# The 64-row tails of the key, value and first dense weights: one load each, from a source that names the rows twice, instead of two loads each

## The chip, the cores and the metric

The kernel runs on one core of a Trainium2 chip. The metric is device microseconds of one execution. Before the change the median of three runs is 150.07 us (149.78 to 150.78).

## What is computed

The input `x` is one sequence of 2048 tokens with 448 features, in bf16. It is normalised, and two branches read the normalised rows; their results are added to `x`.

```
xn  = layernorm(x)
q, k, v = xn @ wqkv                      # 16 heads of 28
phi(t)  = [softmax(t @ w_phi), softmax(-(t @ w_phi))]
kv  = sum_s phi(k)^T v ;  z = sum_s phi(k)
o   = (phi(q) kv) / (phi(q) z + 1e-6)
A   = o @ wo
h   = xn @ w1 + b1                       # w1: 448 x 1792
B   = (h * tanh(softplus(h))) @ w2       # mish
out = x + A + B
```

## The kernel before

**Tokens and features.** The 2048 tokens are 16 tiles of 128 rows, taken in 8 pairs `u`. 448 features are three chunks of 128 and a rest of 64. The transposed rows of a pair, `xnT[:, u]`, have seven chunks: three of the even tile, three of the odd tile, and one (chunk 3) that holds the rest of the even tile in partitions 0 to 63 and the rest of the odd tile in partitions 64 to 127. A matmul against that shared chunk therefore needs the last 64 rows of the weight in both halves of the partitions. Weights are kept as `[128, 4, n]`: chunks 0 to 2 hold rows 0 to 383, and chunk 3 holds rows 384 to 447 twice, once in each half. The projections (`run`, line 433) use one half of the partitions at a time.

**Loads.** `Wkv` is one buffer with the key weights in its first 448 columns and the value weights in the next 448. Rows 0 to 383 come by `load_main` (line 310), `Wk` and `Wv` apart. The last 64 rows, key and value together (64 rows of 1792 bytes), come by `load_tail` (line 315), once for each half. `W1` has the same two parts: `load_main`, and a tail of 64 rows of 3584 bytes for each half. Loads are issued on two queues: SP's (called q1 in the profile) and ACT's (q10). DMA transposes (of `wqkv` into `WqT`, of `xn` into `xnT`, of `Eq` into `EqT`) go through SP's queue too.

**Order.** A list of step names, `ORDER`, sets the order in which the work of all five engines is recorded; each engine runs its own part in that order and waits on semaphores. An engine never runs a later step ahead of one that waits. The steps that matter here are:

- `lba`, `lkma`, `lvma`: the loads of `b1` (14 rows of 256 bytes), of `Wk`'s and of `Wv`'s first 384 rows, on ACT's queue.
- `lktb`: the tail of `Wkv`, lower half on SP's queue and upper half on ACT's.
- `lx1s`, `lx3s`, `lx2s`, `lx4s`, `lx6s`: pieces of `x`; `lps`: `w_phi`; `lqT0` to `lqT3`: transposes of the query weights. All on SP's queue.
- `z5`, `z6`: eleven matmuls of zeros at the start (line 402).
- `wtk0b`, `wtk1b`: TensorE transposes of the key weights (line 585). `wtk0b` reads chunks 0 and 1, `wtk1b` chunks 2 and 3, so it waits for the tail. ACT and DVE each move half of the result out of PSUM; then `wmk0a` and `wmk1a` (line 609) multiply it with `w_phi`.
- `xh3d`, `xh2a`, `xt3a`: TensorE transposes of normalised rows (lines 536 and 520), right behind `wtk1b`.
- `v1Aa`, `v1Ha`: the first projections (line 433); the first of them waits for `Wv`.
- `l1ms`, `l1ts`: `W1`'s main part, and its tail in two loads, both on SP's queue.
- `f0.1H`: the first step of the first dense layer, with chunk 3 of `W1`. It waits for `W1`'s main part and for its tail.

Of the kernel before, what the change touches and what calls it, by code (L numbers as in the profile page):

```python
# [5 lines left out]
ACT = mybir.ActivationFunctionType  # L6
# [6 lines left out]
D = 448  # L13
# [26 lines left out]
class Program:  # L40
# [46 lines left out]
    def dma(self, eng, fn, r=(), w=(), tag=""):  # L87
        return self.op(eng, fn, r, w, dma=True, tag=tag)
# [84 lines left out]
def bass_parallel_sum__linear_kernel_hedgehog__dense_activation_mish__prompt_kernel(  # L173
    nc, A_x, A_wqkv, A_w_phi, A_wo, B_x, B_w1, B_b1, B_w2, out
):
    es = ExitStack()
    with es:
        _kernel(es, nc, A_x, A_wqkv, A_w_phi, A_wo, B_w1, B_b1, B_w2, out)


ORDER = """
zero lx1s lx3s lba st2d lkma lps pw pp st6d lktb lx2s table z5 pi lvma st3a z6 pm lx4s rt3a st7d rs3a xm3a lqT0 rt2p
xm2d b1 xn3d wtk0b bdp wtk1b xh3d st5d xh2a st4d lqT2 xt3a wmk0a wmk1b lqT3 rs2p v1Aa lqT1 st8d v1Ha v3Bd lx6s st9a
v1Ba pk v3Hd k3B xn2d v3Ad rs4p qd k3H xt2m xn4d k3A st14d st15d st12d rs7p lx0s st11d k1H k1A wmq0a wmq1a k1B v2Bd
st13d k2A rs6a k2H v2Ad xn7p st10d q1H xt4m l1ms k2B xn6p v2Hd q1A q2B q1B q2H st1d st0d xt7m q2A e2 v4Ad rs5a v4Hd
# [20 lines left out]
def _kernel(es, nc, A_x, A_wqkv, A_w_phi, A_wo, B_w1, B_b1, B_w2, out):  # L206
    def sb(name, shape, dtype):
        return es.enter_context(nc.sbuf_tensor(name, shape, dtype))
# [21 lines left out]
    W1 = sb("W1", [P, 4, F], BF16)  # L230
# [3 lines left out]
    Wkv = sb("Wkv", [P, 4, 2 * D], BF16)  # L234
# [60 lines left out]
    op, dma = pg.op, pg.dma  # L295
# [4 lines left out]
    HALF = ((0, 64), (64, 128))  # L300
# [9 lines left out]
        dma(eng, lambda e: e.dma_start(dst[:, 0:3, :], src[0:384, :].rearrange("(c p) f -> p c f", p=P)),  # L310
            w=[(name, 0)], tag="ld" + name)

    def load_tail(engs, name, dst, src):
        for i, ((lo, hi), eng) in enumerate(zip(HALF, engs)):
            dma(eng, lambda e, lo=lo, hi=hi: e.dma_start(dst[lo:hi, 3, :], src[384:448, :]),
                w=[("Wt", i) if name == "Wkv" else (name, 1 + i)], tag="ld" + name)

    def load_qT(g, eng):
        dma(eng, lambda e: e.dma_start_transpose(WqT[:, g, 0:D], A_wqkv[:, g * GP:g * GP + P]), w=[("WqT", g)],
# [576 lines left out]
    def add(name, fn, *args):  # L896
        steps[name] = lambda: fn(*args)
# [52 lines left out]
    for eng, c in (("SP", "s"), ("ACT", "a")):  # L950
# [4 lines left out]
        add(f"l1m{c}", load_main, eng, "W1", W1, B_w1)  # L955
        for name, fn in (("p", load_phi), ("b", load_b1), ("2", load_w2), ("o", load_wo)):
            add(f"l{name}{c}", fn, eng)
    for engs, c in ((("SP", "SP"), "s"), (("SP", "ACT"), "b"), (("ACT", "ACT"), "a")):
        add(f"lkt{c}", load_tail, engs, "Wkv", Wkv, A_wqkv[:, D:3 * D])
        add(f"l1t{c}", load_tail, engs, "W1", W1, B_w1)  # L960
    for g in range(G):
        add(f"lqT{g}", load_qT, g, "SP")
    add("b1", bias_T)
# [59 lines left out]
```

## Time and profile before

| | |
|---|---|
| Median of three runs | 150.07 us (149.78 to 150.78) |
| The profiled execution's own time | 149.63 us |
| Its span, first to last instruction | 147.4 us |
| TensorE (PE) busy | 143.1 us, 97% of the span |
| VectorE (DVE) busy | 101.8 us, 69% |
| ScalarE (ACT) busy | 77.0 us, 52% |
| GpSimd (POOL) busy | 39.4 us, 27% |
| DMA, SP's queue (q1) | 38896 packets, 16.09 MB, 51.3% of 16 engines |
| DMA, ACT's queue (q10) | 1052 packets, 0.91 MB, 2.1% of 16 engines |

Some 2.2 us of the execution's own time lie outside the span. A row of the timeline has the start, the length (both in us), the engine, the line of the kernel, the operation, what it writes and reads, and a count; in brackets stands how long the engine was idle before and what ended that. In the chain of waits a row has start, length, and what the end of the program depended on in that time. A DMA row has the packets, the megabytes and the time that the packets took as a share of 16 DMA engines over the stretch asked for.

### The profile page before, as it was taken

The page shows a single profiled execution, that of the slowest core. Times are in us where ns is not written, and L with a number is a line of the kernel's source. Part 1 is how long each engine was busy: PE and PEld are TensorE (multiplying, and loading weights), DVE is VectorE, ACT ScalarE, POOL GpSimd, SP SyncE. Part 2 cuts the span into 40 slices and gives each one's busy share as a digit, 9 for nine tenths or more (in the row PEclk, how much of TensorE's full clock was granted, in tenths as well). Part 3 has the DMA queues.
Part 4 walks back from the last instruction along what each step waited for, and adds up shares of the span by engine and source line. Part 5 has one row for each costly group of instructions (what it writes and reads, how often), then busy time and mean ns, then how long its engine had stood idle before and what let it go on. Part 6 is the DMA issues. An engine that isn't in the chain of part 4 may idle for free.

```text
span 147.4 us, 3868 instructions
## 1 busy us (share of the span) xinstructions
PE 143.1 (97%) x1668; PEld 74.1 (50%) x1668; DVE 101.8 (69%) x227; ACT 77.0 (52%) x98; POOL 39.4 (27%) x54
## 2 busy tenths in 40 slices
PE   7799999999999999999999999999999999999993
PEld 2275555554445545444544446555555545547452
DVE  0898996989997921306999848998997499303522
ACT  3999999989889987996667575000000000000000
POOL 6334283399999990000000000000000000000000
PEclk9999999999999999999999999999999999999999
DMA  4995899995998195399707311015032004500313
GB/s 133 296 274 169 156 350 112 198 202 79 157 203 224 26 163 112 61 190 242 232 4 133 67 32 35 0 24 99 8 57 67 0 4 104 145 0 0 129 64 122
DMA packets 39964, 17.23 MB, mean 117 GB/s; under 512 B 33932, under 2 KB 39180, under 8 KB 39948
## 3 DMA queue, kind: packets, MB, share of 16 engines
q1 hardware_dynamic: 38896, 16.09, 51.3%
q10 hardware_dynamic: 1052, 0.91, 2.1%
q8 instruction: 13, 0.21, 0.6%
q14 instruction: 3, 0.02, 0.0%
HBM read 7.02 MB, written 1.84 MB: 60 GB/s over the span
## 4 chain that ended last, share of the span: by engine, by line
PE 93%; DMA 4%; SPq 1%; DVE 1%; issue 0%
PE PS L433 51%; PE PS L860 29%; PE PS L877 7%; DMA Wkv<-in_A_wqkv_dram 4%; PE PS L754 3%; PE PS L681 2%; PE PS L609 1%; SPq L307 1%; PE PS L585 0%; DVE x_all L824 0%; SPq L330 0%; PE PS L536 0%; PE PS L520 0%; DVE x_all L846 0%
## 5 line engine op out<-in xcount | busy, mean ns | idle before, releaser
L433 PE MATMUL PS<-xnT,W 64*128 64x512 bf16 x392 | 44.8, 376 | 0.0
L860 PE MATMUL PS<-W,actT 128*128 128x448 bf16 (+1 forms) x224 | 42.7, 351 | 0.0
L731 ACT ACTIVATE actT<-PS,b1T 128x1024 bf16<-128x1024 f32 x28 | 30.0, 1113 | 9.3 <-PE PS L433 9.2
L860 PEld LDWEIGHTS PS<-W,actT 128*128 128x128 bf16 x224 | 21.6, 98 | 20.6 <-issue 1.1
L433 PEld LDWEIGHTS PS<-xnT,W 64*128 64x128 bf16 x392 | 18.3, 94 | 21.0 <-issue 0.3
L662 POOL TENSOR_TENSOR actT<-actT,rSk 128x896 bf16<-128x896 bf16 x16 | 26.6, 1700 | 4.8 <-DVE rSk L660 4.8
L824 DVE TENSOR_TENSOR x_all<-PS,x_all 128x448 bf16<-128x448 f32 (+1 forms) x16 | 9.1, 614 | 13.9 <-PE PS L877 8.5
L658 DVE TENSOR_REDUCE Sk<-actT 128x32 f32<-128x896 bf16 x16 | 16.6, 1040 | 0.0
L650 ACT ACTIVATE actT<-PS 128x896 bf16<-128x896 f32 x16 | 13.8, 932 | 0.3 <-PE PS L433 0.2
L433 PE MATMUL PS<-Wkv,xnT 64*128 64x448 bf16 x112 | 13.2, 349 | 0.0
L770 DVE COPY Sq<-PS 128x16 f32<-128x16 f32 x32 | 4.0, 168 | 13.2 <-PE PS L754 13.2
L433 PE MATMUL PS<-Wpk,xnT 64*128 64x448 bf16 x112 | 13.1, 349 | 0.0
L433 PE MATMUL PS<-Wpq,xnT 64*128 64x448 bf16 x112 | 12.7, 349 | 0.0
L471 DVE BATCH_NORM_STATS2 stats<-x_all 128x6 f32<-128x448 bf16 x14 | 8.5, 606 | 3.5 <-DMA x_all<-in_A_x_dram 3.5
L778 DVE TENSOR_TENSOR v_all<-v_all 128x464 f32<-128x464 f32 x16 | 10.3, 643 | 0.6
L774 DVE TENSOR_TENSOR v_all<-PS,Sq 128x464 f32<-128x464 f32 x16 | 10.3, 641 | 0.5
L781 DVE TENSOR_TENSOR xn<-v_all,rden 128x448 bf16<-128x448 f32 x16 | 10.0, 625 | 0.6
L776 DVE TENSOR_TENSOR v_all<-PS,Sq 128x464 f32<-128x464 f32 x16 | 10.1, 630 | 0.0
L712 ACT ACTIVATE actT<-PS 128x896 bf16<-128x896 f32 x10 | 8.4, 925 | 0.6 <-PE PS L433 0.5
L527 DVE CAST v_all<-PS 128x896 bf16<-128x896 f32 x6 | 6.5, 1080 | 3.0 <-PE PS L433 3.0
L433 PEld LDWEIGHTS PS<-Wkv,xnT 64*128 64x128 bf16 x112 | 5.4, 94 | 5.0
L433 PEld LDWEIGHTS PS<-Wpq,xnT 64*128 64x128 bf16 x112 | 5.4, 94 | 5.1 <-ACT actT L731 0.2
(85 smaller groups left out, 121.0 us busy)
## 6 DMA issues: line engine op xcount, KB each, us to landing
W<-in_B_w_dram SPq DMA_DIRECT2D x1, 1568.0 KB, 8.2
out_dram<-x_all SPq DMA_DIRECT2D x7, 224.0 KB, 2.2
W<-in_B_w_dram SPq DMA_DIRECT2D x1, 1344.0 KB, 6.8
x_all<-in_A_x_dram SPq DMA_DIRECT2D x4, 224.0 KB, 2.9
x_all<-in_A_x_dram SPq DMA_DIRECT2D x2, 448.0 KB, 5.1
Wkv<-in_A_wqkv_dram ACTq DMA_DIRECT2D x2, 336.0 KB, 5.1
Wo<-in_A_wo_dram SPq DMA_DIRECT2D x2, 336.0 KB, 4.3
W<-in_B_w_dram SPq DMA_DIRECT2D x2, 224.0 KB, 3.6
```

The source lines that it names most:

```text
L433: ins = e.matmul(o, lhs(c, k), rhs(c, k), start=first and n == at[par][0], stop=last and n == at[par][-1])
L650: op("ACT", lambda e, s=s: e.activation(E_of(u)[:, s, :, :], two(b, D), ACT.Exp, scale=1.0 if s == 0 else -1.0), r=[pb(b), pb(b + 1)], w=[ ...
L658: op("DVE", lambda e: e.tensor_reduce(Sk[u][:, s, :], Eh(), AX.X, ALU.add), r=[("E", u, s)], w=[("Sk", u, s)], tag=f"Sk{u}.{s}")
L662: op("POOL", lambda e: e.tensor_tensor(Eh(), Eh(), ap_on(rSk[u][:, s, 0:1], [[1, 2 * H], [0, DH]]), ALU.mult), r=[("E", u, s), ("rSk", u, ...
L731: op("ACT", lambda e: e.activation(actT[:, fc, q * 1024:(q + 1) * 1024], bank(b, 2), ACT.Mish, bias=b1T[:, fc:fc + 1]), r=[("b1T",), pb(b) ...
L774: op("DVE", lambda e: e.tensor_tensor(tv(t1[i]), num(0), sx(1), ALU.mult), r=[pb(b), pb(b + 1), ("Sq", i, 1)], w=[("t1", i)], tag=f"ta{t}")
L776: op("DVE", lambda e: e.tensor_tensor(tv(t2), num(1), sx(0), ALU.mult), r=[pb(b), pb(b + 1), ("Sq", i, 0)], w=[("t2",)], tag=f"tb{t}")
L778: op("DVE", lambda e: e.tensor_tensor(t1[i], t1[i], t2, ALU.add), r=[("t1", i), ("t2",)], w=[("t1", i)], tag=f"tc{t}")
L781: op("DVE", lambda e: e.tensor_tensor(o_sb[(t // 2) % 2][:, t % 2, :].rearrange("p (h d) -> p h d", d=DH), t1[i][:, :, 0:DH], ap_on(rden[i ...
L824: op("DVE", lambda e: e.tensor_tensor(x_all[:, t, 0:n], bank(b)[:, 0:n], x_all[:, t, 0:n], ALU.add), r=[pb(b), ("x", t)], w=[("out", t)], ...
L860: ins = e.matmul(bank(b)[:, 0:width(t)], actT[:, fc, tok(t)], W2[:, fc, 0:width(t)], start=first and fc == 0, stop=last and fc == FC - 1)
L877: ins = e.matmul(bank(b)[:, 0:w], oT_of(u)[lo:hi, cc * P:(cc + 1) * P], Wo[lo:hi, cc, 0:w], start=first and n == at[par][0], stop=last and ...
```

## The change

The tail of a weight is loaded by one DMA that writes all 128 partitions. Its source has three dimensions, 2 by 64 by the row, and the step of the first is zero, so that the same 64 rows are read twice. The destination has 128 partitions as its first dimension. `Wkv`'s tail is now issued by ACT alone (`lkta` in the place of `lktb`), and `W1`'s, as before, by SP.

```diff
-zero lx1s lx3s lba st2d lkma lps pw pp st6d lktb lx2s table ...
+zero lx1s lx3s lba st2d lkma lps pw pp st6d lkta lx2s table ...

-    def load_tail(engs, name, dst, src):
-        for i, ((lo, hi), eng) in enumerate(zip(HALF, engs)):
-            dma(eng, lambda e, lo=lo, hi=hi: e.dma_start(dst[lo:hi, 3, :], src[384:448, :]),
-                w=[("Wt", i) if name == "Wkv" else (name, 1 + i)], tag="ld" + name)
+    def load_tail(eng, name, dst, src):
+        rows = src[384:448, :]
+        twice = bass.AP(tensor=rows.tensor, offset=rows.offset, ap=[[0, 2]] + [list(d) for d in rows.ap])
+        dma(eng, lambda e: e.dma_start(dst[:, 3, :], twice),
+            w=[("Wt", 0), ("Wt", 1)] if name == "Wkv" else [(name, 1), (name, 2)], tag="ld" + name)

-    for engs, c in ((("SP", "SP"), "s"), (("SP", "ACT"), "b"), (("ACT", "ACT"), "a")):
-        add(f"lkt{c}", load_tail, engs, "Wkv", Wkv, A_wqkv[:, D:3 * D])
-        add(f"l1t{c}", load_tail, engs, "W1", W1, B_w1)
+    for eng, c in (("SP", "s"), ("ACT", "a")):
+        add(f"lkt{c}", load_tail, eng, "Wkv", Wkv, A_wqkv[:, D:3 * D])
+        add(f"l1t{c}", load_tail, eng, "W1", W1, B_w1)
```

Lines below the changed function are numbered one higher after the change. ACT's first instructions, at the start of the program, before the change (the size is that of the destination):

```order
L334 DMA b_rows<-in_B_b_dram 14x128
L310 DMA Wkv<-in_A_wqkv_dram 128x3x448
L315 DMA Wkv<-in_A_wqkv_dram 64x896
L348 ACT_TABLE_LOAD
L310 DMA Wkv<-in_A_wqkv_dram 128x3x448
```

The same place after it:

```order
L335 DMA b_rows<-in_B_b_dram 14x128
L310 DMA Wkv<-in_A_wqkv_dram 128x3x448
L316 DMA Wkv<-in_A_wqkv_dram 128x1x896
L349 ACT_TABLE_LOAD
L310 DMA Wkv<-in_A_wqkv_dram 128x3x448
```

The tail stands in the same place of ACT's queue, behind `Wk`'s main part and ahead of `Wv`'s, with twice the partitions. On SP's queue the load `Wkv<-in_A_wqkv_dram 64x896`, which stood between `w_phi` and the third piece of `x`, is gone, and everything behind it moves up by one place.

TensorE at the transposes of the key weights, before, with the semaphores that each waits for (`dma_61` is `Wk`'s main part, `dma_62` the upper half of the tail, `dma_3` the lower half):

```order
L585 MATMUL PS<-ident,Wkv 112x128 [waits dma_61]
L585 MATMUL PS<-ident,Wkv 112x128 x7
L585 MATMUL PS<-ident,Wkv 112x128 [waits dma_62,dma_3]
L585 MATMUL PS<-ident,Wkv 112x128 x7
L536 MATMUL PS<-ident,xn 128x128 [waits done_DVE,done_ACT]
```

After (`dma_59` is the main part, `dma_60` the one load of the tail):

```order
L586 MATMUL PS<-ident,Wkv 112x128 [waits dma_59]
L586 MATMUL PS<-ident,Wkv 112x128 x7
L586 MATMUL PS<-ident,Wkv 112x128 [waits dma_60]
L586 MATMUL PS<-ident,Wkv 112x128 x7
L537 MATMUL PS<-ident,xn 128x128 [waits done_DVE,done_ACT]
```

The order of TensorE's work is the same; `wtk1b` (the third row) waits for one load in place of two.

SP's queue around `W1`'s tail, before:

```order
L546 DMA_TRANSPOSE xnT<-xn 128x7x128 x2
L720 DMA_TRANSPOSE EqT<-actT 128x8x128
L546 DMA_TRANSPOSE xnT<-xn 128x7x128
L315 DMA W<-in_B_w_dram 64x1792 x2
L720 DMA_TRANSPOSE EqT<-actT 128x8x128 x2
```

After:

```order
L547 DMA_TRANSPOSE xnT<-xn 128x7x128 x2
L721 DMA_TRANSPOSE EqT<-actT 128x8x128
L547 DMA_TRANSPOSE xnT<-xn 128x7x128
L316 DMA W<-in_B_w_dram 128x1x1792
L721 DMA_TRANSPOSE EqT<-actT 128x8x128 x2
```

One issue takes the place of two, at the same point between the transposes. The first matmul of the first dense layer (`f0.1H`) waited for three loads, the main part and two tails, and now waits for two.

More of the change, by code (lines that the diff above doesn't have):

```diff
@@ L181 @@
 ORDER = """
-zero lx1s lx3s lba st2d lkma lps pw pp st6d lktb lx2s table z5 pi lvma st3a z6 pm lx4s rt3a st7d rs3a xm3a lqT0 rt2p
+zero lx1s lx3s lba st2d lkma lps pw pp st6d lkta lx2s table z5 pi lvma st3a z6 pm lx4s rt3a st7d rs3a xm3a lqT0 rt2p
 xm2d b1 xn3d wtk0b bdp wtk1b xh3d st5d xh2a st4d lqT2 xt3a wmk0a wmk1b lqT3 rs2p v1Aa lqT1 st8d v1Ha v3Bd lx6s st9a
```

## The prediction

> **What bounds the kernel now.** The page comes first: its first line and the shares of the chain that ended last.
>
> ```profile
> PE 143.1 (97%) x1668; PEld 74.1 (50%) x1668; DVE 101.8 (69%) x227; ACT 77.0 (52%) x98; POOL 39.4 (27%) x54
> PE 93%; DMA 4%; SPq 1%; DVE 1%; issue 0%
> ```
>
> TensorE is the bound, and the only other sizeable share is one transfer. The chain of waits, in order of time, says which (start, length, what):
>
> ```profile
> 1.74 0.42 SPq L330
> 2.20 5.20 DMA Wkv<-in_A_wqkv_dram
> 7.44 0.65 PE PS L585 x8
> ...
> 15.40 34.03 PE PS L433 x348
> ```
>
> The lower half of `Wkv`'s tail, issued by SP at 2.20, lands at 7.40 and releases `wtk1b` at 7.44. From there to the last matmul the chain is TensorE almost alone: what delays `wtk1b` delays the end, and TensorE has no later slack to win it back. The timeline of TensorE around that point:
>
> ```profile
> 0.96 4.87 PE L402 MATMUL PS<-zeros 128*128 128x512 bf16 x11 [0.96 <-POOL zeros L354]
> 5.76 0.18 PE L725 MATMUL PS<-ident,b_rows 14*128 14x14 bf16 x1
> 6.19 0.65 PE L585 MATMUL PS<-ident,Wkv 128*112 128x128 bf16 x8 [0.25 <-DMA Wkv<-in_A_wqkv_dram]
> 7.44 0.65 PE L585 MATMUL PS<-ident,Wkv 128*112 128x128 bf16 x8 [0.60 <-DMA Wkv<-in_A_wqkv_dram]
> ...
> 9.60 2.25 PE L433 MATMUL PS<-Wkv,xnT 64*128 64x448 bf16 x22
> ```
>
> TensorE waits 0.60 us for the tail today, so an earlier tail can win at most 0.6 us there. `W1`'s tail is not in the chain. Its issue, its landing and its first use (SP's timeline, the DMA issues, TensorE's timeline) say how near it is:
>
> ```profile
> 30.17 1.23 SPq L315 DMA_DIRECT2D W<-in_B_w_dram  x2
> W<-in_B_w_dram SPq DMA_DIRECT2D x2, 224.0 KB, 3.6
> 35.77 7.72 PE L433 MATMUL PS<-xnT,W 64*128 64x512 bf16 x70
> ```
>
> The second of the two loads is issued at about 30.8 and lands 3.6 us later, near 34.4. `f0.1H` wants it at 35.77. The slack is 1.4 us.
>
> **How many DMA engines a load gets.** The change gives the two tails a source whose first dimension is 2, where every load before leads with its rows. So I ask what the first dimension does. Packets on a queue in a stretch with one or two loads tell it. Here are ACT's queue from 0 to 3 us (`b1` alone, 14 rows), ACT's queue from 145.8 to 147 (the last store, 128 rows), and SP's queue from 31.5 to 34.2 (`W1`'s tails, twice 64 rows):
>
> ```profile
> L725 PE MATMUL PS<-ident,b_rows x1: 177/177/177, 5.8 to 5.8; 14*128 14x14 bf16 x1
> q10 hardware_dynamic: 28, 0.00, 0.8%
> q10 hardware_dynamic: 144, 0.10, 24.5%
> q1 hardware_dynamic: 160, 0.46, 68.8%
> ```
>
> Rows taken off, 14, 16 and 32 packets are left: each transfer ends with one small packet for each DMA engine that took part. The 128-row and the 64-row transfers had 16 engines, the 14-row one had 14. The engines are thus dealt out along the first dimension, equal shares each. A source that leads with 2 can be dealt to two engines only, one copy of 64 rows each, unless the destination's 128 partitions alone decide. No row of before shows a transfer whose sides lead with different counts. Two engines is what I take as likeliest.
>
> The Trainium skill (DMA: Bandwidth & Descriptors, "Why a DMA increments its semaphore by 16 and not by 1" and "Rules for kernel authors") says that the number of engines is the largest up to 16 that divides the slowest dimension of both sides, and that a leading zero-stride broadcast of c copies confines the DMA to at most c engines. The 14 finishing packets agree; the repeated source is shown by no run here. The same list of rules advises one 128-partition transfer in place of two halves, which speaks for the change; by that line alone the time would stay at 150.
>
> **The change part by part.** The sum is made against the profiled execution, 149.63 us (span 147.4); the median of the runs is 0.4 above it.
>
> *Issues.* One issue fewer on SP at the start and one fewer at `W1`. In the row above two issues took 1.23 us, so one is worth 0.6. It moves the loads of `x` and the transposes behind it up by 0.6 us. None of them is in the chain, so I count 0. One semaphore fewer at `wtk1b` and `f0.1H`: 0. The bytes are the same.
>
> *`Wkv`'s tail on two engines.* Each engine carries 64 rows of 1792 bytes, 114.7 KB, where an engine carried 4 rows for each half before. The pace of an engine has two ends. From 5.6 to 7.9 both queues are busy; from 20 to 21.8 there are only the 3584-byte packets of `W1`'s main part:
>
> ```profile
> q1 hardware_dynamic: 237, 0.43, 56.3%
> q10 hardware_dynamic: 389, 0.33, 49.2%
> q1 hardware_dynamic: 195, 0.70, 100.4%
> ```
>
> ACT's queue moved 0.33 MB in 2.3 us on 16 engines, 9.0 GB/s for one engine that it shares with SP's queue. Alone, SP's moved 0.70 MB in 1.8 us, 24.2 GB/s for an engine. The tail thus takes between 114.7/24.2 = 4.7 us and 114.7/9.0 = 12.7 us. When it starts comes from the upper half of before:
>
> ```profile
> Wkv<-in_A_wqkv_dram ACTq DMA_DIRECT2D x1, 112.0 KB, 4.8
> 1.95 0.53 ACTq L315 DMA_DIRECT2D Wkv<-in_A_wqkv_dram  x1
> ```
>
> It landed at 1.95 + 4.8 = 6.75, and its 7.2 KB an engine took 0.8 us at 9.0 GB/s. So the ring is free for the tail at 5.95, counted so that the landing is included. The bounds are 10.7 and 18.7. How long the sharing lasts is set by SP's queue, whose last transpose of the query weights is issued at 7.84 and lands 3.8 us later, at 11.6:
>
> ```profile
> 7.84 1.27 SPq L319 DMA_TRANSPOSE WqT<-in_A_wqkv_dram  x1
> WqT<-in_A_wqkv_dram SPq DMA_TRANSPOSE x1, 3.8
> ```
>
> Until 11.6 the shared pace brings 5.7 x 9.0 = 51 KB; the other 63 KB take 2.6 us at the free pace. The tail lands at 14.2, and `wtk1b` starts **6.8 us later** than at 7.44 (bounds 3.3 to 11.3). `Wv`'s main part stands behind the tail in the same two rings: 21.5 KB each, 0.9 us, landed at 15.1. The first projection wants it 2.16 us after `wtk1b` (7.44 to 9.60), at 16.4, so it stays hidden by 1.3 us. Behind `wtk1b` on TensorE stands everything. On ACT and DVE the moves of its result out of PSUM stand ahead of most statistics and normalisations, so these shift along and the rest of the program moves as a block.
>
> *`W1`'s tail on two engines.* Each carries 64 packets of 3584 bytes. At the free pace a packet takes 1.8 x 16 x 1.004 / 195 = 0.148 us; in the stretch from 31.5 to 34.2 it took 2.7 x 16 x 0.688 / 128 = 0.232 us. That is 9.5 us or 14.9 us. I take 9.5: nothing else is on ACT's queue then, and two engines ask less of the memory than sixteen. Of the 3.6 us of before, 4 packets at 0.232 are 0.9, so 2.6 to 2.7 are there whatever the size. The load lands at 30.17 + 2.6 + 9.5 = 42.3, counted in the times of before, against 35.77 wanted: **6.5 us** of waiting (bounds: 4.5 if it is issued 2 us early against TensorE, 11.9 at the slow pace). It is a second stall and not cover for the first, if SP issues the load as late as TensorE is late. That is so where SP waited for ACT's exponentials of TensorE's results shortly before (waits of SP's queue, and its timeline):
>
> ```profile
> SPq L720 <- ACT actT L712: 8.3, 3, 4.5
> 22.61 1.23 SPq L720 DMA_TRANSPOSE EqT<-actT  x1
> ```
>
> From 22.61 to 31.4 SP issues back to back. The `EqT` transposes that follow on SP's queue also wait behind the tail in the two rings, but their first use is a later stage.
>
> *TensorE after an idle stretch.* The eleven 512-column matmuls at the start took 4.87 us, 443 ns each; in the row at 35.77 a pair of half-height ones takes 2 x 7.72/70 = 220 ns. The start cost 11 x 223 ns = 2.45 us of half pace after idleness. No row shows how long an idle stretch must be, so each of the two stalls costs 0 to 2.45. The first one's restart runs 2.16 us in step with ACT and DVE anyway, which leaves 2.45 x (4.87 - 2.16)/4.87 = 1.4; of the second, with the shorter idle, I count half, 1.2. Together **2.6 us** (bounds 0 and 4.9).
>
> The Trainium skill (TensorE: Matmul & The Clock Gate, Part 1) says that the clock halves after an idle window of about 3.4 us and returns after about as long under load. Both stalls would then cost about 1.7 us each, 3.4 in place of 2.6; the 4.87 us of half pace at the start agree in kind.
>
> *Sum:* 149.6 + 6.8 + 6.5 + 2.6 = 165.5 for the profiled execution, and 0.4 more for the median: **166 us**.
>
> **The rivals.** (1) *The destination decides: sixteen engines.* Then the tail is one load on ACT's queue with 112 KB more: at 16 x 9.0 GB/s that is 0.8 us behind 6.75, so 7.5 against 7.40, and `W1`'s tail is as hidden as before. Time 150.0, between 149.4 (all of the 0.6 us won) and 150.7. For it: the destination leads with 128, like most loads. Against: equal dealing needs a count that fits both sides. This is also the case in which the change does no more than it says. 12%. Faster by over 1% would need 1.5 us, more than the 0.6 us of waiting.
>
> (2) *Two engines, but `W1`'s tail is hidden*, because SP gets ahead of TensorE by 6.5 us or more: 166 - 6.5 - 1.2 = 158.3. Against it speaks SP's wait ahead of 22.61. 7%.
>
> (3) *Two engines at the slow pace throughout*, with both idle stretches charged in full: 150.0 + 11.3 + 11.9 + 4.9 = 178. For it: the memory may be slow for one engine as well. Against: 24.2 GB/s is what each engine reached with fifteen others busy. 5%.
>
> **How the numbers follow.** The forecast has 75%, the rivals 12, 7 and 5, and 1% is left for what I don't see. The forecast's own bounds come from its two landings: 157.5 (tail at 10.7, `W1` waiting 4.5, no slow clock: 150.0 + 3.3 + 4.5 = 157.8) to 173 (one of the two terms near its far end). That range takes in rival 2; rivals 1 and 3 and a little more are left out. Within 1% is about what a measurement of this kernel can tell from no change: 11% for that, 1% faster, 88% slower.
>
> **What would show it.** In the profile after, the tail's load should have a landing of some 12 us instead of 5, and TensorE should idle before `wtk1b` until about 14 us; `W1`'s tail should take about 12 us to land with a second idle stretch of 5 to 8 us before `f0.1H`; matmuls behind each at twice their length show the clock. Landings of 5 and 3.6 us would prove rival 1. The forecast is wrong if the tails are dealt to sixteen engines, or if one of the two stalls is missing.

## The result, and the profile after

The changed kernel takes **167.17 us** (median of 6 runs, 165.6 to 167.59) against 149.95 us for six runs of before: a ratio of 1.113, 95% interval 1.109 to 1.118. The forecast was 166. The profiled execution took 167.45 us, with a span of 165.2 against 147.4: 17.8 us more.

The page's first line and the shares of the chain, after:

```profile
PE 147.7 (89%) x1668; PEld 77.2 (47%) x1668; DVE 102.0 (62%) x227; ACT 77.3 (47%) x98; POOL 39.4 (24%) x54
PE 84%; DMA 6%; issue 4%; ACT 3%; ACTq 1%; DVE 0%
```

TensorE has the same 1668 matmuls and is busy for 89% of the span instead of 97%. Where it stood idle is read from the chain and from TensorE's timeline. The chain (start, length, what):

```profile
1.96 10.73 DMA Wkv<-in_A_wqkv_dram
12.73 1.10 PE PS L586 x8
...
42.41 3.25 ACT actT L651 x4
45.66 5.71 issue
51.37 15.90 PE PS L434 x132
```

The timeline of TensorE, with the idle time and its releaser in brackets:

```profile
6.05 0.65 PE L586 MATMUL PS<-ident,Wkv 128*112 128x128 bf16 x8 [0.59 <-DMA Wkv<-in_A_wqkv_dram]
12.73 1.10 PE L586 MATMUL PS<-ident,Wkv 128*112 128x128 bf16 x8 [6.03 <-DMA Wkv<-in_A_wqkv_dram]
...
42.94 0.92 PE L434 MATMUL PS<-Wpk,xnT 64*128 64x448 bf16 x8
51.37 9.96 PE L434 MATMUL PS<-xnT,W 64*128 64x512 bf16 x70 [7.51 <-issue]
```

`wtk1b` waits 6.03 us for `Wkv`'s tail and starts at 12.73 instead of 7.44. `f0.1H` waits 7.51 us. The chain names ACT and "issue" for that second wait and not the load, and the reason is itself part of the finding. The DMA issues of the two tails:

```profile
Wkv<-in_A_wqkv_dram ACTq DMA_DIRECT2D x1, 224.0 KB
W<-in_B_w_dram SPq DMA_DIRECT2D x1, 448.0 KB
38.31 0.70 SPq L316 DMA_DIRECT2D W<-in_B_w_dram  x1
```

Both rows lack a time to landing. That time is taken where a load's semaphore has been raised 16 times. The trace shows three raises for each of these loads: for `Wkv`'s tail at 3.02, 12.53 and 12.69 us, for `W1`'s at 39.42, 51.24 and 51.27. One comes soon after the issue and two with the data, as many as the DMA engines that the packets below count. `W1`'s tail, issued at 38.31, landed at 51.27, and `f0.1H` started at 51.37. The packets on ACT's queue tell the same:

```profile
q10 hardware_dynamic: 1102, 1.02, 1.9%
```

Without the tail that queue carries 28 packets for `b1`, 400 each for `Wk` and `Wv` and 144 for the last store, 972. The tail has 130: 128 rows and **two finishing packets**. Before, its upper half had 1052 - 972 = 80, 64 rows and 16.

The clock, by stretches (length, busy time of each engine, then PEclk, DMA share and GB/s):

```profile
5.60:8.10 2.50, 0.65 (x8) 0.51 (x8) 2.12 (x9) 2.29 (x7) 1.11 (x2) 1.00 1.06 346
8.20:18.30 10.10, 5.57 (x48) 4.51 (x50) 3.85 (x11) 4.00 (x8) 1.41 (x3) 0.50 0.96 107
18.40:49.00 30.60, 25.46 (x276) 12.97 (x270) 26.21 (x57) 26.13 (x37) 19.07 (x21) 1.00 0.95 133
49.10:55.90 6.80, 4.54 (x22) 1.91 (x24) 5.18 (x8) 0.05 (x1) 6.80 (x5) 0.50 0.93 137
56.00:60.00 4.00, 4.00 (x40) 2.02 (x38) 0.00 (x0) 2.08 (x2) 2.13 (x2) 1.00 0.96 176
```

The granted clock falls to half in the course of each wait, at 8.12 and 49.08 us, and stays there for some microseconds of work behind it. The same work from `wtk1b` to the query weights, 106 matmuls in a row without idleness, in before and after:

```profile
7.44:15.40 7.96, 7.96 (x106) 5.30 (x108) 7.21 (x20) 7.42 (x14) 3.02 (x7) 1.00 0.92 208
12.73:23.32 10.59, 10.59 (x106) 7.25 (x108) 6.66 (x18) 7.29 (x13) 2.34 (x5) 0.73 0.66 87
```

It costs 2.6 us more, and the 70 matmuls from `f0.1H` on take 9.96 instead of 7.72, 2.2 us more. So the added 17.8 us are 12.73 - 7.44 = 5.3 for the first wait, 2.6 for the clock behind it, 7.5 for the second wait, 2.2 for the clock behind that, and 0.2 of rest.

### The profile page after: what moved, and what is told of

The parts are those of the page before. It is cut to its first block, busy times and chain, and to the rows that moved or that the text cites. A ratio compares the mean times of both kernels' runs of the same rounds, so it can differ in the third digit from the quotient of the medians.

```text
span 165.2 us, 3864 instructions
## 1 busy us (share of the span) xinstructions
PE 147.7 (89%) x1668; PEld 77.2 (47%) x1668; DVE 102.0 (62%) x227; ACT 77.3 (47%) x98; POOL 39.4 (24%) x54
## 4 chain that ended last, share of the span: by engine, by line
PE 84%; DMA 6%; issue 4%; ACT 3%; ACTq 1%; DVE 0%
PE PS L434 45%; PE PS L861 26%; DMA Wkv<-in_A_wqkv_dram 6%; PE PS L878 6%; PE PS L755 2%; ACT actT L651 2%; PE PS L610 1%; PE PS L682 1%; ACT actT L713 1%; PE PS L586 1%; PE PS L521 0%; PE PS L537 0%; ACTq L335 0%; DVE x_all L825 0%; ACTq L310 0%
## 5 line engine op out<-in xcount | busy, mean ns | idle before, releaser
L434 PE MATMUL PS<-xnT,W 64*128 64x512 bf16 x392 | 47.0, 390 | 7.5 <-issue 7.5
L434 PEld LDWEIGHTS PS<-xnT,W 64*128 64x128 bf16 x392 | 19.3, 97 | 30.0 <-issue 10.9
L825 DVE TENSOR_TENSOR x_all<-PS,x_all 128x448 bf16<-128x448 f32 (+1 forms) x16 | 9.1, 612 | 13.9 <-PE PS L878 8.5
L434 PE MATMUL PS<-Wkv,xnT 64*128 64x448 bf16 x112 | 14.0, 366 | 0.0
L771 DVE COPY Sq<-PS 128x16 f32<-128x16 f32 x32 | 4.0, 167 | 13.2 <-PE PS L755 13.2
```

Source lines behind the costliest of these rows:

```text
L434: ins = e.matmul(o, lhs(c, k), rhs(c, k), start=first and n == at[par][0], stop=last and n == at[par][-1])
```

## The experiments

The theory: a load gets as many DMA engines as divide the first dimension of both its sides, so two here; each tail stalls TensorE on its own; and idleness halves the clock. The rivals: reading the same rows twice is slow; one load or one queue in place of two is slow; the second stall only follows from the first; what follows a stall is slow because ACT and DVE restart too.

### The first dimension, with and without repetition

Four forms of the one load, each on the queues of after. `lead2` takes two different blocks of 64 rows, `lead8` eight blocks of 16, `lead128` 128 consecutive rows, and `repeat128` one row 128 times.

```diff
-        rows = src[384:448, :]                       # after: [[0, 2], [row, 64], [1, n]]
+        rows = src[256:448, :]                       # lead2
+        twice = bass.AP(..., ap=[[128 * step, 2], [step, 64], list(run)])
+        rows = src[264:448, :]                       # lead8
+        twice = bass.AP(..., ap=[[24 * step, 8], [step, 16], list(run)])
+        twice = src[320:448, :]                      # lead128
+        rows = src[384:385, :]                       # repeat128
+        twice = bass.AP(..., ap=[[0, 128], list(rows.ap[-1])])
```

> As after, but the source takes two different blocks of 64 rows (256 to 319 and 384 to 447), so it still leads with 2 and repeats nothing; the lower half of the tail gets other rows than the reference's. Theory (the leading 2 gives two engines): as after, 167 us (165 to 169), landings of 11 and 13 us. Rival (reading the same addresses twice is what is slow): both halves are read once, so 150 us.

> As after, but the source is 8 blocks of 16 rows, 24 rows apart, so it leads with 8; most of the tail gets other rows than the reference's. Theory (engines by the leading count): eight engines with 16 rows each. Wkv's tail takes between 28.7/24.2 = 1.2 us and 28.7/9.0 = 3.2 us, lands at 7.2 to 9.1; W1's takes 2.6 + 16 x 0.148 = 5.0 us and stays hidden: 150.8 us (149.5 to 152). Rival (any source of three dimensions is served slowly): 167 us.

> One load for each tail on the same queues as after, from 128 consecutive rows (320 to 447), so that both sides lead with 128; the lower half of the tail gets other rows than the reference's. Theory (engines by the leading count): sixteen engines, the tail lands near 7.5 us and W1's tail in 3.5 us: 150.0 us (149.3 to 150.8). Rival (one load in place of two, or one queue in place of two, is what is slow): 160 us or more.

> One load for each tail on the queues of after, whose source is row 384 read 128 times (first step zero, count 128); all rows of the tail get that row's values. Theory (engines by the leading count, whatever its step): sixteen engines, 150 us (149 to 151). Rival (a zero step or re-reading is slow): 158 us or more.

| First dimension of the source | Time | Ratio to before, 95% |
|---|---|---|
| 2, rows repeated (after) | 167.17 us | 1.113 (1.109 to 1.118) |
| 2, no row repeated | 166.42 us | 1.106 (1.095 to 1.116) |
| 8, no row repeated | 154.67 us | 1.029 (1.020 to 1.038) |
| 128, no row repeated | 150.90 us | 1.002 (0.998 to 1.006) |
| 128, one row repeated | 152.09 us | 1.012 (1.002 to 1.021) |

Each ratio is to runs of before that were made beside it (medians of 149.95 to 150.63 us). The times with 2 (no row repeated), 8 and one row repeated are of two runs each.

ACT's queue on the pages of `lead2`, `lead8`, `lead128` and `repeat128`, in that order:

```profile
q10 hardware_dynamic: 1102, 1.02, 1.9%
q10 hardware_dynamic: 1108, 1.02, 2.4%
q10 hardware_dynamic: 1116, 1.02, 2.4%
q10 hardware_dynamic: 1116, 1.02, 2.4%
```

Less 972 and 128 rows, 2, 8, 16 and 16 finishing packets are left: the number of engines is the first dimension of the source, up to 16, with the destination at 128 throughout. How long TensorE's chain waited for the tail (start, length) in the same order:

```profile
1.96 11.27 DMA Wkv<-in_A_wqkv_dram
1.97 7.29 DMA Wkv<-in_A_wqkv_dram
1.96 6.37 DMA Wkv<-in_A_wqkv_dram
1.96 6.55 DMA Wkv<-in_A_wqkv_dram
```

Repetition is not what is slow: without it the two-engine load costs as much, and with it the sixteen-engine load has the same span as `lead128` in the profiles (149.1 us) and is within about 1% of it in the runs. Nor is it the three-dimensional form: `lead8` has it too, and takes 154.67 us and not 167. The Trainium skill (DMA: Bandwidth & Descriptors, "Why a DMA increments its semaphore by 16 and not by 1") gives the rule of the largest divisor up to 16; 2, 8, 14 and 16 finishing packets agree with it.

My expectation for `lead8`, 150.8, was too low by 4 us. The tail landed 1.9 us later than before, and I had forgotten the clock. The timeline and the clock of `lead8`:

```profile
9.30 1.10 PE L587 MATMUL PS<-ident,Wkv 128*112 128x128 bf16 x8 [2.87 <-DMA Wkv<-in_A_wqkv_dram]
8.20:14.90 6.70, 5.60 (x48) 4.53 (x50) 3.70 (x10) 4.00 (x8) 2.44 (x5) 0.50 1.02 188
```

The clock fell during these 2.87 us of idleness: the eight transposes take 1.10 us instead of 0.65, and the clock is half for about 6.8 us. The span is 4.6 us longer than before, 1.9 of it the wait and the rest the clock's: the 106 matmuls from `wtk1b` on take 10.70 us here, 7.96 before.

### One tail at a time

```diff
-        add(f"l1t{c}", load_tail, eng, "W1", W1, B_w1)
+        add(f"l1t{c}", load_tail2, (eng, eng), "W1", W1, B_w1)                       # wkv_only
-        add(f"lkt{c}", load_tail, eng, "Wkv", Wkv, A_wqkv[:, D:3 * D])
+        add(f"lkt{c}", load_tail2, ("SP", "ACT"), "Wkv", Wkv, A_wqkv[:, D:3 * D])    # w1_only
```

Here `load_tail2` is the function of before, two loads of 64 rows.

> The one-load form for Wkv's tail alone; W1's tail comes by two loads as before. Theory (a load gets as many DMA engines as divide the first dimension of both its sides, two here, and each tail stalls TensorE by itself): the tail lands near 12.7 us, TensorE waits 5.3 us more ahead of wtk1b, its clock is half for some 5.6 us after it, which costs 2.6, and W1's tail lands in time: 150.0 + 5.3 + 2.6 = 157.9 us (157 to 159). Rival (the second stall is a follow-up of the first, since everything behind it is late): most of the 17 us stay, 165 or more.

> The one-load form for W1's tail alone; Wkv's tail comes by two loads as before. Theory (two engines, each tail stalls by itself): the load is issued near 30.2 us and takes 13 us, so it lands near 43.1 where 35.8 is wanted; 7.4 us of idleness and 2.2 us of half clock behind it: 159.6 us (158 to 161). Rival (the second stall is a follow-up of the first): 150 to 152.

With `Wkv`'s tail alone in the new form the time is 157.89 us (ratio 1.049, 1.041 to 1.057), with `W1`'s alone 158.82 (1.056, 1.049 to 1.063). Each tail costs its share by itself, 4.9% and 5.6%, which make 10.5 of the 11.3% of both together. TensorE at `f0.1H` in `wkv_only` and in `w1_only`:

```profile
44.53 7.72 PE L439 MATMUL PS<-xnT,W 64*128 64x512 bf16 x70
43.60 9.91 PE L439 MATMUL PS<-xnT,W 64*128 64x512 bf16 x70 [7.34 <-issue]
```

In the first there is no idleness and the clock is full, although the step comes nearly 9 us later than before. In the second there are 7.34 us of idleness and 2.2 us of slow clock, with the start of the kernel as before. The rival in which the second stall follows from the first is out.

### Keeping TensorE busy through the waits

```diff
-xm2d b1 xn3d wtk0b bdp wtk1b xh3d ...
+xm2d b1 xn3d wtk0b bdp z12 z12 wtk1b xh3d ...
-... v5Bd k0A k0H f0.1H kn3.1
+... v5Bd k0A k0H z12 z12 z10 f0.1H kn3.1
```

> As after, with 24 matmuls of zeros on TensorE ahead of wtk1b and 34 ahead of f0.1H, which fill most of the two idle stretches (24 x 0.22 = 5.3 us and 34 x 0.22 = 7.5 us) and change no result. Theory (the time behind each stall is the clock, halved by idleness): the clock stays full and 2.6 + 2.2 = 4.8 us go, 167.2 - 4.8 = 162.4 us (161.5 to 163.5). Rival (what follows a stall is slow because ACT and DVE restart with it): 167 us or a little more.

163.33 us, a ratio of 1.085 (1.078 to 1.092) where after has 1.113: some 4 us less for 58 useless matmuls. TensorE's timeline, and the stretch with its clock:

```profile
6.51 5.41 PE L403 MATMUL PS<-zeros 128*128 128x512 bf16 x24
13.69 0.65 PE L586 MATMUL PS<-ident,Wkv 128*112 128x128 bf16 x8 [1.77 <-DMA Wkv<-in_A_wqkv_dram]
5.70:20.00 14.30, 12.40 (x116) 7.08 (x117) 7.22 (x21) 7.58 (x18) 3.36 (x7) 1.00 1.00 140
```

The clock stays at 1.00, and the eight transposes take 0.65 us again. The gain is not all of the 4.8 us. `Wkv`'s tail landed at 13.65 here, at 12.69 in the profile of after; and `W1`'s tail landed at 48.61, but the matmuls of zeros held TensorE until `f0.1H` at 49.74. The time behind the stalls was the clock's, not ACT's or DVE's.

### Hiding the slow load

Here `Wkv`'s tail comes by two loads, and `W1`'s by the two-engine load, issued on ACT's queue well ahead of its use.

```diff
-zero lx1s lx3s lba st2d lkma lps pw pp st6d lkta lx2s table z5 pi lvma st3a ...
+zero lx1s lx3s lba st2d lkma lps pw pp st6d lkta lx2s table z5 pi lvma l1ta st3a ...      # w1_early
-... k1A wmq0a wmq1a k1B ...
+... k1A wmq0a wmq1a l1ta k1B ...                                                            # w1_mid
-... e3 xt0m l1ts k7B ...
+... e3 xt0m k7B ...                                                                         # both
-        add(f"lkt{c}", load_tail, eng, "Wkv", Wkv, A_wqkv[:, D:3 * D])
+        add(f"lkt{c}", load_tail2, ("SP", "ACT"), "Wkv", Wkv, A_wqkv[:, D:3 * D])           # both
```

> Wkv's tail by two loads as before; W1's tail by the one load of two engines, but issued early, on ACT's queue behind Wv's main part (near 3 us). Theory (a slow load costs only what it is late): it lands before 25 us, 10 us ahead of its use: 150 us (149.3 to 151.0). Rival (two engines filled for 10 us delay what shares their rings or engines, the pieces of x and the transposes that the layer norm and the projections wait for): 152 us or more.

> As the run with the early load (Wkv's tail by two loads, W1's by the one load of two engines on ACT's queue), but issued later, behind the query weights' results on ACT, near 17 us, when the query weights' transposes have landed. Theory (a load on two engines costs what it is late, plus what it slows on the same two engines): it takes 13 to 17 us and lands at 30 to 34, ahead of its use at 35.8; what it can slow are the transposes of the normalised rows, which are needed less soon: 150 to 153 us. Rival (whatever shares the two engines is late wherever the load stands): 155 us or more.

159.94 us (1.064, 1.057 to 1.071) and 158.89 us (1.057, 1.052 to 1.063). Both expectations missed; the rivals were right. In both, `W1`'s tail was there in time (20.0 and 27.7 us by its last raise). In `w1_early` the query weights' transposes, spread over all engines on the other queue, were late; TensorE's timeline and the DMA issues:

```profile
22.83 1.68 PE L615 MATMUL PS<-Wbd,WqT 112*128 112x112 bf16 x16 [6.53 <-DVE WqT L329]
WqT<-in_A_wqkv_dram SPq DMA_TRANSPOSE x4, 13.5
```

Before, these transposes landed after 5.1 us. In `w1_mid` it was the transposes of the normalised rows, and `W1`'s main part (TensorE's timeline, the transposes' times to landing, and the DMA issues):

```profile
28.07 1.68 PE L439 MATMUL PS<-Wkv,xnT 64*128 64x448 bf16 x8 [6.52 <-DMA xnT<-xn]
DMA to landing us min/median/max: 3.1/3.8/12.7
W<-in_B_w_dram SPq DMA_DIRECT2D x1, 1344.0 KB, 15.4
```

The same two rows in before; the slowest transpose took a third of the time:

```profile
DMA to landing us min/median/max: 2.9/3.2/4.0
W<-in_B_w_dram SPq DMA_DIRECT2D x1, 1344.0 KB, 6.8
```

One such transpose landed at 27.93, just after `W1`'s tail. Behind each of the two waits the clock was at half for 6.8 us, as in after, which is the other part of the price.

How a load on two engines holds up the others stays open. One reading is that a transfer spread over 16 engines has landed when its slowest engine is through, and two of the 16 were full. The semaphores say that there is more to it. In `w1_mid` `W1`'s main part, a plain load over sixteen engines, has its sixteen raises between 32.09 and 32.24, over 4 us after the two-engine load had landed at 27.72; had only two engines been held up, the other raises would have come early. The transpose ahead of it in SP's queue has all of its own between 27.75 and 27.93. So all of SP's queue was late, and not its share on two engines alone. Which engine a packet ran on is not in the trace. Nor does any run issue the same 448 KB over sixteen engines at these places, so the part of the two engines in the delay isn't separated from that of the bytes.

### Both halves on one queue, in two loads

```diff
-zero lx1s lx3s lba st2d lkma lps pw pp st6d lktb lx2s table ...
+zero lx1s lx3s lba st2d lkma lps pw pp st6d lkta lx2s table ...      # before's own load_tail, ("ACT", "ACT")
```

> Before, with both 64-row halves of Wkv's tail issued by ACT, two loads one behind the other; sixteen engines each; W1's tail as before. Theory (half of the pace of an engine goes to each queue, so 112 KB more on ACT's queue land 0.9 us later whether in one load or in two): TensorE starts wtk1b near 8.4 instead of 7.4 as with the 128-row load, 150.5 to 151.5 us. Rival (the 128-row load is itself slower than two of 64 rows): the tail lands at 7.4, 150.0 us.

The ratio is 1.011 (1.003 to 1.019); the profiled run took 151.73 us, a little above the 150.5 to 151.5 expected. The tail's second half landed at 7.80 and `wtk1b` started at 7.84, between the two expectations (8.4 and 7.4), so this run does not settle whether 128 rows in one load are slower than two loads of 64. It shows that moving both halves to ACT's queue wins nothing. The clock makes up a part of the price here too: it fell 1.7 us after TensorE's last matmul and stayed at half for 3.4 us:

```profile
7.84 1.10 PE L585 MATMUL PS<-ident,Wkv 128*112 128x128 bf16 x8 [1.77 <-DMA Wkv<-in_A_wqkv_dram]
7.80:11.20 3.40, 3.36 (x33) 3.36 (x34) 3.19 (x9) 2.56 (x5) 0.39 (x1) 0.50 1.24 300
```

In `warm` the same 1.77 us of idleness ahead of the same step left the clock full, so the length of the idle time alone does not decide it.

No form tried here was faster than before.

## Why the prediction was right, step by step

- **Two engines.** The step that decided the sign held: the 14 finishing packets of the 14-row load suggested the rule, and 2, 8 and 16 confirmed it. That load leads with 14 on both sides, so by the rows of before alone the destination might have decided, as the prediction said; `lead8` and `lead128`, with the same destination, settled it. The rival of sixteen engines is what `lead128` and `repeat128` show, 150.9 and 152.1.
- **First wait, 6.8 forecast, 5.3 measured.** The tail landed at 12.7 and not 14.2. Two parts of this term were off. Its first packet went at 4.70, where I had the ring free at 5.95. And the pace was not 9.0 GB/s until the last query transpose at 11.6. Here are SP's and ACT's queues in after from 9 to 12 us:

```profile
q1 hardware_dynamic: 572, 0.14, 128.6%
q10 hardware_dynamic: 72, 0.13, 11.1%
```

These 72 packets are rows of the tail: 72 x 1792 bytes in 3 us on two engines are 21.5 GB/s for each, near the free pace, although SP's queue was busy with transposes until 14.83. Up to 9.0 the tail had moved 54 rows at 11.3 GB/s. In the profiles of the other runs with this load the landing varies from 13.2 to 13.9. `Wv` behind the tail stayed hidden, as worked out.

- **Second wait, 6.5 forecast, 7.5 measured.** The load took 38.31 to 51.27, 13.0 us instead of 12.1. The pace was as forecast: the median packet took 0.140 us where I took 0.148. What I had not counted is a pause: two packets that went at 39.95 took 1.65 us each, and the next followed at 41.59; in `w1_only` such a pair took 1.93 us. No run shows what held them. SP issued the load 5.6 us ahead of TensorE's need in before and after alike, so it was as late as TensorE was, and `w1_only` showed a second stall and not cover for the first, as said.
- **Clock, 2.6 forecast, 4.8 measured.** The kind was right, the size was the worst term: I discounted the first restart because it runs in step with ACT and DVE (1.4, measured 2.6), and halved the second for doubt (1.2, measured 2.2). The prediction's estimate from the Trainium skill's page was 3.4.
- **Issues and semaphores, 0 forecast.** Nothing of them is seen in the 0.2 us of rest.

The sum was 15.9 and the span grew by 17.8; the first wait was too long by 1.5, the other terms too short by 1.0 and 2.2. That 166 came so near to 167.2 is thus in part luck: the errors had both signs.

## What to carry to other kernels

Before two loads are merged into one with a broadcast source, look at the first dimension of both sides: it decides over how many DMA engines the bytes go, and two engines took 10.7 us for what sixteen, in two loads, brought in 5.2. Issuing the slow load early did not make it harmless in the two places tried: one transpose beside it took 12.7 us to land, where the slowest of before took 4.0. And where a wait of some microseconds stands ahead of dense matmuls, add the price of the half clock behind it, here 2.2 to 2.6 us for each of the two in after.

## What was not expected of the hardware

Behind the first wait the clock fell sooner than I had thought. In after it went to half at 8.12 us, 1.4 us after TensorE's last matmul, and in `act_two` 1.7 us after it, while 1.63 us of idleness in `lead128` and 1.77 us in `warm` left it alone. The Trainium skill (TensorE: Matmul & The Clock Gate, Part 1) speaks of an idle window of about 3.4 us. The trace's changes of the clock do come in steps of that size (half from 8.12 to 18.36, three times 3.41, and from 49.08 to 55.91, twice). At the second wait the fall agrees with the page: the 3.41 us up to 49.08 held no matmul, while the 3.41 us before them held 1.60 us and left the clock full; it fell 5.2 us after the last matmul. At the first wait it does not: the 3.41 us from 4.71 to 8.12 held 1.40 us of matmuls, and the clock fell at their end.

The amount of work in such a window does not decide the early falls alone either. In `w1_early` the one from 4.59 to 8.00 held 1.80 us of matmuls and the clock fell; in `lead128` the one from 6.35 to 9.76 held 1.78 us and it stayed full. What does decide them stays open.

A slow load also made others slow: in `w1_mid` `W1`'s main part took 15.4 us instead of 6.8 beside a two-engine load of a third of its size.
